# RWKV-6 attention with a mixture-of-depths layer: row shifts issued by ScalarE, another layout of the exponentials, another order on TensorE

## The chip, the cores and the metric

The kernel runs on one core of a Trainium2 chip. The metric is the device time of one launch in microseconds (us), from start to end on that core; lower is better. A profile of one execution lies beside the times. In it PE is TensorE, PEld its weight loads, DVE VectorE, ACT ScalarE, POOL GpSimd, SP SyncE; "L205" is line 205 of the kernel before, and "SPq" is the time that SP's queue spends on issuing DMAs.

## The reference

Two layers follow each other. The first is a linear attention with a decay for each channel (4 batches, 8 heads, 768 steps, 48 channels per head), the second lets the 128 best-scored rows of each batch through a small MLP (384 to 1024 to 384):

```python
for t in range(S):
    cur = np.einsum('bhd,bhe->bhde', u[None] * kt, vt)
    y[:, :, t] = np.einsum('bhd,bhde->bhe', rt, state + cur)
    state = wt[:, :, :, None] * state + np.einsum('bhd,bhe->bhde', kt, vt)
...
scores = np.einsum('bsd,d->bs', x, w_gate)
for b in range(B):
    top_idx = np.argpartition(-scores[b], capacity)[:capacity]
    xe = x[b, top_idx]
    ye = np.maximum(xe @ w1, 0.0) @ w2
    g = 1.0 / (1.0 + np.exp(-scores[b, top_idx]))
    out[b, top_idx] = x[b, top_idx] + g[:, None] * ye
```

Here x is y with the heads side by side: 384 columns.

## The kernel before

**Chunks.** The 768 steps of a batch are cut into 6 chunks of 128 steps, so there are 24 chunks, numbered 0 to 23 over the batches. The 128 steps lie on the partitions. For each chunk `load` (L107) fetches w, k, r and v with one DMA each, 192 KB in runs of 48 numbers.

**What is computed for a chunk.** `lnw` (L137, ACT) takes the logarithm of the decays. `sums` (L146) multiplies it on PE with a triangular matrix, which gives sums from each step to the end of the chunk; ACT then makes `fall` = exp(sum) (L149) and `rise` = exp(-sum) (L160). `scaled` (L205, DVE) needs `rise` for r, and for k it needs `e`: the rows of `fall` moved up by one step. For the first three chunks `e` is made by a second product (L155, L156); for all others two DMAs copy rows 1 to 112 and 113 to 127 of `fall` to the partitions below (L159, issued by SP). `turned` (L216 PE, L218 ACT) transposes k and r; `scores` (L233), `fresh` (L249), `from_state` (L292) and `from_chunk` (L310) are the products proper. They use quarters of the PE array: 16 products of at most 64 x 64 each, twice 16 instructions since fp32 takes two passes. `masked` (L261), `states` (L274 to L281) and `result` (L332, L338, L342) close the chunk on DVE, POOL and SP.

**The whole decay.** The first row of `fall` holds the decay over the whole chunk. The state of the next chunk is scaled by it (L281, POOL), so it has to stand on the partitions, one channel each. `line` (L166) sends that row to DRAM, and `whole` (L174) fetches it back in two DMAs of 48 x 4 single numbers.

**The order.** The program is one loop over turns n = -4 ... 23 (L532), written out by hand; each engine executes its part in the order of the text. One turn works on several chunks: loads of chunk n+7, `sums` of n+4, `scaled` of n+3, `turned` of n+2, `scores` to `states` of n+1, `from_state` and `from_chunk` of n, `result` of n-1. SP's queue in a turn is: four loads, in turns 0 to 6 one DMA with MLP weights (L537), two of `whole`, one of `result` (which waits for DVE's L332), two shifts, one of `line`. All quarter products of a chunk go to one of two PSUM buffers (`ps_p`), so `scores(n+1)` has to wait until `result(n-1)` has read the other use of that buffer. `fall` lies in two buffers in turn, so `fall` of chunk n+4 waits until the DMAs that read `fall` of chunk n+2 are done. In the compiled program the DMAs share eight completion semaphores, and an issue waits until the earlier DMA on its semaphore has landed.

**The MLP.** `mixture` (L347 on) is a generator of 28 steps per batch; while a batch's 6 turns run, the steps of the batch before it are dealt out, 4 or 5 per turn (`per_turn`, L485), half of them after `line` and half at the end of the turn. Steps: two halves of a transposed score row (`every`, L354, L357), six comparisons (`ahead`, L367), the choice of rows and their gather (L376 to L410), the transposed rows (`xeT`, L418, L420), the gate (L425 to L441), eight steps of the first product (L449; after the fourth and eighth, ACT's `hid`, L454), eight of the second (L459, then `ye`, L465). All its PSUM tiles share one buffer (pool `psM`). The MLP of the last batch runs alone at the end (L561).

Of the kernel before, what the change touches and what calls it, by code (L numbers as in the profile page):

```python
# [9 lines left out]
FP32 = mybir.dt.float32  # L10
# [3 lines left out]
AF = mybir.ActivationFunctionType  # L14
# [3 lines left out]
L = 128  # L18
HB = 64
# [17 lines left out]
def kernel(  # L37
# [14 lines left out]
    nc = tc.nc  # L52
# [27 lines left out]
    N = len(chunks)  # L80
    views = dram_disjoint_views(out, B)

    lines = dram.tile([N, C], FP32, name="lines")
    score = consts.tile([L, B, NCH], FP32)
    guard = consts.tile([L, N, 2], FP32)
    w1 = consts.tile([L, NDC, F], FP32)
# [2 lines left out]
    wg_bc = consts.tile([L, C], FP32)  # L89
    k_bufs = [consts.tile([L, H, HB], FP32, name=f"k_buf{i}") for i in range(4)]  # L90
    r_bufs = [consts.tile([L, H, HB], FP32, name=f"r_buf{i}") for i in range(3)]
    e_bufs = [consts.tile([L, C], FP32, name=f"e_buf{i}") for i in range(3)]
    p_bufs = [psP.tile([L, 2, 512], FP32, name=f"ps_p{i}") for i in range(2)]
    all_bufs = [consts.tile([L, HP], FP32, name=f"all_buf{i}") for i in range(6)]

# [37 lines left out]
    def lnw(n):  # L133
        if 0 <= n < N:
# [3 lines left out]
                out=t["lw"], in_=t.pop("w").rearrange("p h d -> p (h d)"), func=AF.Ln  # L138
            )

    def sums(n):
        if not 0 <= n < N:
            return
        t = work[n]
        ps = psR.tile([L, 512], FP32, tag="r", name="ps_x")
        nc.tensor.matmul(ps[:, 0:C], tri, t["lw"], start=True, stop=True)  # L146
        fall = t["fall"] = lev.tile([L, C], FP32, tag="fall", name="fall")
        rise = t["rise"] = lev.tile([L, C], FP32, tag="rise", name="rise")
        after[n - 4] = nc.scalar.activation(  # L149
            out=fall, in_=ps[:, 0:C], func=AF.Exp, accum_out=guard[:, n, 0:1]  # L150
        )
        e = t["e"] = e_bufs[n % len(e_bufs)]
        if n < EARLY:
            strict = psR.tile([L, 512], FP32, tag="r", name="ps_x")
            nc.tensor.matmul(strict[:, 0:C], tri_s, t["lw"], start=True, stop=True)  # L155
            nc.scalar.activation(out=e, in_=strict[:, 0:C], func=AF.Exp)  # L156
        else:
            for lo, hi in ((0, L - 16), (L - 16, L - 1)):
                nc.sync.dma_start(out=e[lo:hi], in_=fall[lo + 1:hi + 1])  # L159
        nc.scalar.activation(  # L160
            out=rise, in_=ps[:, 0:C], func=AF.Exp, scale=-1.0, accum_out=guard[:, n, 1:2]
        )

    def line(n):
        if 0 <= n < N:
            nc.sync.dma_start(out=lines[n:n + 1], in_=work[n]["fall"][0:1])  # L166

    def whole(n):
        if not 0 <= n < N or chunks[n][1] == 0:
            return  # L170
        t = work[n]["all"] = all_bufs[n % len(all_bufs)]
        line = lines[n].rearrange("(j q d) -> q d j", q=2, d=D)
        for par in (0, 1):
            nc.sync.dma_start(out=t[HB * par:HB * par + D, :], in_=line[par])  # L174
# [16 lines left out]
    def own_values(n):  # L191
        if not 0 <= n < N:
            return
        t = work[n]
        t["vo"] = lev.tile([L, H, D], FP32, tag="vo", name="vo")
        nc.gpsimd.tensor_mul(t["vo"], t["v"], t.pop("own").to_broadcast([L, H, D]))  # L196

    def scaled(n):
        if not 0 <= n < N:
            return  # L200
        t = work[n]
        t["K"] = k_bufs[n % len(k_bufs)]
        t["R"] = r_bufs[n % len(r_bufs)]
        for to, of, by in (("K", "k", "e"), ("R", "r", "rise")):
            nc.vector.tensor_mul(  # L205
                t[to][:, :, 0:D], t.pop(of), t.pop(by).rearrange("p (h d) -> p h d", d=D)
            )

    def turned(n):
        if not 0 <= n < N:  # L210
            return
        t = work[n]
        for name in "KR":
            ps = psR.tile([L, HP, L], FP32, tag="r", name="ps_t")
            for j in range(HP):
                nc.tensor.transpose(ps[:, j, :], t[name][:, 2 * j:2 * j + 2, :], ident)  # L216
            t[name + "t"] = lev.tile([L, HP, L], FP32, tag=name + "t", name=name + "t", bufs=3)
            nc.scalar.copy(out=t[name + "t"], in_=ps)  # L218
        t.pop("R")

    quarters = [(par, sub) for par in (0, 1) for sub in (0, 1)]

# [3 lines left out]
    def scores(n):  # L226
        if not 0 <= n < N:
            return
        t = work[n]
        P = t["P"] = p_bufs[n % 2]  # L230
        for j in range(HP):
            for par, sub in quarters:
                nc.tensor.matmul(  # L233
                    P[half(sub), par, j * HB:(j + 1) * HB],
                    t["Kt"][half(par, D), j, half(sub)], t["Rt"][half(par, D), j, half(sub)],
                    start=True, stop=True,
                )
        t.pop("Kt")
# [44 lines left out]
    def from_state(n):  # L283
        if not 0 <= n < N:
            return
        t = work[n]
        begun = set()
        for j in range(HP):
            for par, sub in quarters:
                if sub == 0 and chunks[n][1] == 0:  # L290
                    continue
                nc.tensor.matmul(  # L292
                    t["P"][half(sub), par, j * D:(j + 1) * D],
                    t["Rt"][half(par, D), j, half(sub)],
                    t["s1" if sub else "s0"][half(par, D), j, :],
                    start=(par, sub) not in begun, stop=False, skip_group_check=True,
                )
                begun.add((par, sub))
# [182 lines left out]
    def mix(n):  # L481
        for _ in range(n):
            next(mixing, None)
# [4 lines left out]
    with tc.manual_schedule():  # L488
# [20 lines left out]
        nc.vector.tensor_tensor(out=ident, in0=col, in1=row, op=ALU.is_equal)  # L509
        for t in k_bufs + r_bufs:  # L510
            nc.vector.memset(t[:, :, D:HB], 0.0)
        for t in all_bufs:
            nc.gpsimd.memset(t, 1.0)
        nc.vector.tensor_tensor(out=behind[:, 0:L], in0=col, in1=row, op=ALU.is_lt)
        for i in (0, 1):
            nc.vector.tensor_copy(out=mask[half(i)], in_=behind[half(i), half(i)])
# [15 lines left out]
        for n in range(-4, N):  # L532
            if n > -4:
                load(n + AHEAD)
            if n >= 0 and n < len(weights):
                to, of = weights[n]
                nc.sync.dma_start(out=to, in_=of)  # L537
            whole(n + 3)
            result(n - 1)
            if n > 0 and chunks[n][1] == 0:  # L540
                mixing = run(mixing, mixture(chunks[n][0] - 1))
            pieces = per_turn[chunks[n][1]] if n >= NCH else 0
            lnw(n + 4)
            turned(n + 2)
            from_state(n)
            own_products(n + 3)
            own_values(n + 1)
            sums(n + 4)
            line(n + 4)
            mix(pieces // 2)  # L550
            scaled(n + 3)
            own_sum(n + 2)
            scores(n + 1)
            fresh(n + 1)
            masked(n + 1)
            states(n + 1)
            from_chunk(n)
            mix(pieces - pieces // 2)
        result(N - 1)
        mixing = run(mixing, mixture(B - 1))  # L560
        mix(1000)  # L561
# [81 lines left out]
```

## Time and profile before

| | |
|---|---|
| median of 3 runs | 267.96 us (266.21 to 270.43) |
| the profiled execution | 270.15 us |
| its span in the profile | 268.2 us |
| PE, PEld busy | 198.0, 154.3 us |
| DVE busy | 142.7 us |
| POOL busy | 101.2 us |
| ACT busy | 74.5 us |
| mean granted PE clock | 0.837 of full speed |
| DMA moved | 33.50 MB in 117347 packets, 109491 of them under 512 B |
| K product (L205, DVE) of chunk 3, 9, 15, 21 starts at | 35.53, 83.22, 134.13, 186.13 us |
| last product of the last chunk (L310) ends, about | 231 us |

The busy share of an engine is an average over stages: up to about 84 us the loads and weights fill the DMA queues, then three batches of about 52 us each carry the MLP of the batch before, and from 233 us on the last MLP stands alone. The start times of the K products mark the turns (chunk m is scaled in turn m-3), so they show what each stage costs.

### The profile page before, as it was taken

How to read it: one execution, taken by the hardware profiler on the slowest of the kernel's cores; microseconds unless marked ns; L12 is line 12 of the kernel's file. 1: busy time of each engine (PE TensorE's matmuls, PEld its weight loads, DVE VectorE, ACT ScalarE, POOL GpSimd, SP SyncE). 2: the span in 40 equal slices, each digit the busy share in tenths (PEclk: the TensorE clock that was granted, in tenths of full speed). 3: DMA queues.
4: the chain of work that ended last, by engine and by line, in shares of the span. 5: the costliest groups of instructions: out<-in, count | busy, mean ns of one | idle time of the engine just before them, and what ended most of it. 6: DMA issues, size and time to landing. Idle time of an engine off the chain costs nothing.

```text
span 268.2 us, 8468 instructions
## 1 busy us (share of the span) xinstructions
PE 198.0 (74%) x3592; PEld 154.3 (58%) x3592; DVE 142.7 (53%) x330; ACT 74.5 (28%) x200; POOL 101.2 (38%) x119
## 2 busy tenths in 40 slices
PE   3728557859958859889986698899746988824880
PEld 1416446646747647777765497666535986413740
DVE  7324054345655966576499586566994633271010
ACT  3506313233233312441352134433502110000100
POOL 5350422555414642573175524814735220101001
PEclk9995956795696866999997679999995799955995
DMA  7999779879878867776586746612122001011001
GB/s 146 196 200 200 142 168 229 199 199 240 210 155 199 200 147 166 178 149 139 119 196 151 172 107 144 139 32 91 32 61 62 32 18 46 12 47 33 0 0 42
DMA packets 117347, 33.50 MB, mean 125 GB/s; under 512 B 109491, under 2 KB 116534, under 8 KB 117302
## 3 DMA queue, kind: packets, MB, share of 16 engines
q1 hardware_dynamic: 116790, 31.31, 52.1%
q0 software_dynamic: 512, 1.57, 1.8%
q8 instruction: 30, 0.49, 0.8%
q14 instruction: 15, 0.12, 0.1%
HBM read 23.23 MB, written 5.54 MB: 107 GB/s over the span
## 4 chain that ended last, share of the span: by engine, by line
PE 42%; DVE 17%; SPq 13%; DMA 12%; issue 7%; ACT 5%; POOL 0%; DVEq 0%; POOLq 0%; ACTq 0%
PE ps_f L459 9%; SPq L107 9%; PE ps_h L449 8%; DMA e_buf<-fall 7%; DVE ahead L367 5%; PE ps_p L310 5%; PE ps_t L216 4%; PE ps_x L146 4%; PE ps_p L233 4%; PE ps_p L292 4%; DMA xe<-out_dram,idx 2%; DVE sc L261 2%; PE ps_p L249 2%; SPq L174 2%; ACT rise L160 2%
## 5 line engine op out<-in xcount | busy, mean ns | idle before, releaser
L281 POOL TENSOR_TENSOR s<-mid,all_buf 128x192 f32<-128x192 f32 x20 | 12.1, 603 | 96.3 <-PE ps_p L310 24.5
L205 DVE TENSOR_TENSOR k_buf<-k,e_buf 128x384 f32<-128x384 f32 x24 | 20.8, 868 | 43.6 <-DMA e_buf<-fall 33.4
L218 ACT COPY Kt<-ps_t 128x512 f32<-128x512 f32 x24 | 14.1, 586 | 95.8 <-PE ps_t L216 95.8
L310 PE MATMUL ps_p<-v,sc 64*64 64x48 f32 x768 | 32.9, 240 | 2.7 <-issue 2.5
L261 DVE TENSOR_TENSOR sc<-ps_p,mask 128x512 f32<-128x512 f32 x24 | 16.4, 685 | 32.0 <-PE ps_p L249 32.0
L310 PEld LDWEIGHTS ps_p<-v,sc 64*64 64x64 f32 x768 | 30.4, 157 | 3.8 <-issue 3.4
L146 PE MATMUL ps_x<-lw,tri 128*128 128x384 f32 x48 | 27.9, 670 | 5.7 <-ACT lw L137 5.7
L181 POOL TENSOR_TENSOR rk<-r,k 128x384 f32<-128x384 f32 x24 | 28.6, 1193 | 6.4 <-DVE own L189 4.3
L449 PE MATMUL ps_h<-xeT,w 128*128 128x128 f32 x192 | 27.3, 295 | 3.9 <-ACT hid L454 2.7
L182 POOL TENSOR_TENSOR rk<-rk,u_bc 128x384 f32<-128x384 f32 x24 | 26.3, 1095 | 6.2 <-DMA u_bc<-in_u_dram 4.4
L449 PEld LDWEIGHTS ps_h<-xeT,w 128*128 128x128 f32 x192 | 24.8, 204 | 6.6 <-ACT hid L454 3.2
L459 PE MATMUL ps_f<-w,hid 128*128 128x384 f32 x64 | 23.9, 504 | 3.3 <-ACT hid L454 2.6
L233 PEld LDWEIGHTS ps_p<-Rt,Kt 48*64 48x64 f32 x768 | 16.8, 165 | 16.5 <-issue 9.1
L196 POOL TENSOR_TENSOR vo<-v,own 128x384 f32<-128x384 f32 x24 | 24.4, 1015 | 4.4 <-DVE x L332 4.4
L233 PE MATMUL ps_p<-Rt,Kt 48*64 48x64 f32 x768 | 20.6, 259 | 4.0 <-DVE x L332 4.0
L216 PE MATMUL ps_t<-ident,r_buf 128*128 128x128 f32 x96 | 19.2, 335 | 5.8 <-ACT e_buf L156 5.8
L216 PE MATMUL ps_t<-ident,k_buf 128*128 128x128 f32 x96 | 18.7, 327 | 6.4 <-DVE k_buf L205 6.4
L149 ACT ACTIVATE fall<-ps_x 128x384 f32<-128x384 f32 x24 | 11.8, 490 | 38.1 <-PE ps_x L146 23.8
L292 PE MATMUL ps_p<-s,Rt 48*64 48x48 f32 x704 | 18.5, 242 | 4.1 <-DVE mid L279 4.1
L292 PEld LDWEIGHTS ps_p<-s,Rt 48*64 48x64 f32 x704 | 15.5, 154 | 9.9 <-issue 7.9
L367 DVE SCALAR_TENSOR_TENSOR ahead<-every,score,behind 128x768 bf16<-128x768 f32 (+5 forms) x24 | 19.8, 868 | 1.2 <-ACT every L357 1.2
L205 DVE TENSOR_TENSOR r_buf<-r,rise 128x384 f32<-128x384 f32 x24 | 18.8, 783 | 0.0
(79 smaller groups left out, 263.1 us busy)
## 6 DMA issues: line engine op xcount, KB each, us to landing
w<-in_w_dram SPq DMA_DIRECT2D x24, 192.0 KB
k<-in_k_dram SPq DMA_DIRECT2D x24, 192.0 KB
r<-in_r_dram SPq DMA_DIRECT2D x24, 192.0 KB
v<-in_v_dram SPq DMA_DIRECT2D x24, 192.0 KB
out_dram<-x SPq DMA_DIRECT2D x24, 192.0 KB
e_buf<-fall SPq DMA_DIRECT2D x21, 168.0 KB
w<-in_moe_w_dram SPq DMA_DIRECT2D x3, 512.0 KB
w<-in_moe_w_dram SPq DMA_DIRECT2D x4, 384.0 KB
```

What stands on the lines that cost most here:

```text
L146: nc.tensor.matmul(ps[:, 0:C], tri, t["lw"], start=True, stop=True)
L181: nc.gpsimd.tensor_mul(rk, t["r"], t["k"])
L182: nc.gpsimd.tensor_mul(rk, rk, u_bc)
L196: nc.gpsimd.tensor_mul(t["vo"], t["v"], t.pop("own").to_broadcast([L, H, D]))
L205: nc.vector.tensor_mul(t[to][:, :, 0:D], t.pop(of), t.pop(by).rearrange("p (h d) -> p h d", d=D))
L216: nc.tensor.transpose(ps[:, j, :], t[name][:, 2 * j:2 * j + 2, :], ident)
L233: nc.tensor.matmul(P[half(sub), par, j * HB:(j + 1) * HB], t["Kt"][half(par, D), j, half(sub)], t["Rt"][half(par, D), j, half(sub)], start ...
L292: nc.tensor.matmul(t["P"][half(sub), par, j * D:(j + 1) * D], t["Rt"][half(par, D), j, half(sub)], t["s1" if sub else "s0"][half(par, D), ...
L310: ins = nc.tensor.matmul(t["P"][half(sub), par, j * D:(j + 1) * D], t["sc"][half(sub), par, j, :], t["v"][half(sub), 2 * j + par, :], star ...
L367: nc.vector.scalar_tensor_tensor(out=ahead[:, c, lo:S], in0=every[:, lo:S], scalar=score[:, b, c:c + 1], in1=behind[:, 0:S - lo], op0=ALU. ...
L449: nc.tensor.matmul(ps[:, q, :], w1[:, dc, (f0 + q) * L:(f0 + q + 1) * L], xeT[:, dc, :], start=(dc == 0), stop=(dc == NDC - 1),)
L459: nc.tensor.matmul(ps, hid[:, fc, :], w2[:, fc, :], start=(fc == 0), stop=(fc == NFC - 1))
```

## The change

There are three parts.

1. **Shifts from ScalarE.** The two DMAs that shift `fall` into `e` are issued by ACT, after `rise`; ACT's queue holds them between `rise` and what follows.
2. **Another layout of `fall` and `e`.** Both are stored as [parity of the head, channel, head pair] with 64 channel rows, of which 16 hold ones: a channel's four head pairs lie side by side. Row 0 is then, number by number, what the 128 partitions need, 4 each: `whole` becomes one DMA from SBUF to SBUF of 128 x 4 numbers, with no trip through DRAM, and comes at the end of the same turn in place of `line`. ACT writes `fall` and DVE reads `e` in steps of 16 bytes; a shifted row is two runs of 768 bytes instead of one of 1536. `fall` lies in two fixed buffers.
3. **Another order.** In a turn PE now has: transposes of K, `from_state`, transposes of R, `scores`, `sums`, a third of the MLP steps, `fresh`, a third, `from_chunk`, the rest. Before it was: both transposes, `from_state`, `sums`, half of the steps, `scores`, `fresh`, `from_chunk`, the rest.

```diff
-    lines = dram.tile([N, C], FP32, name="lines")
-    e_bufs = [consts.tile([L, C], FP32, name=f"e_buf{i}") for i in range(3)]
+    fall_bufs = [consts.tile([L, 2, HB, HP], FP32, name=f"fall_buf{i}") for i in range(2)]
+    e_bufs = [consts.tile([L, 2, D, HP], FP32, name=f"e_buf{i}") for i in range(3)]
...
+    def natural(ap):
+        return ap.rearrange("p q d j -> p j q d")
...
         after[n - 4] = nc.scalar.activation(
-            out=fall, in_=ps[:, 0:C], func=AF.Exp, accum_out=guard[:, n, 0:1]
+            out=natural(fall[:, :, 0:D, :]),
+            in_=ps[:, 0:C].rearrange("p (j q d) -> p j q d", q=2, d=D),
+            func=AF.Exp, accum_out=guard[:, n, 0:1],
         )
+        nc.scalar.activation(
+            out=rise, in_=ps[:, 0:C], func=AF.Exp, scale=-1.0, accum_out=guard[:, n, 1:2]
+        )
...
             for lo, hi in ((0, L - 16), (L - 16, L - 1)):
-                nc.sync.dma_start(out=e[lo:hi], in_=fall[lo + 1:hi + 1])
-        nc.scalar.activation(
-            out=rise, in_=ps[:, 0:C], func=AF.Exp, scale=-1.0, accum_out=guard[:, n, 1:2]
-        )
-    def line(n):
-        if 0 <= n < N:
-            nc.sync.dma_start(out=lines[n:n + 1], in_=work[n]["fall"][0:1])
+                nc.scalar.dma_start(out=e[lo:hi], in_=fall[lo + 1:hi + 1, :, 0:D, :])
...
-        line = lines[n].rearrange("(j q d) -> q d j", q=2, d=D)
-        for par in (0, 1):
-            nc.sync.dma_start(out=t[HB * par:HB * par + D, :], in_=line[par])
+        nc.sync.dma_start(out=t, in_=work[n]["fall"][0:1].rearrange("o q d j -> o (q d j)"))
...
+        nc.vector.tensor_mul(
+            t["K"][:, :, 0:D].rearrange("p (j q) d -> p j q d", q=2),
+            t.pop("k").rearrange("p (j q) d -> p j q d", q=2), natural(t.pop("e")),
+        )
...
-        for t in all_bufs:
-            nc.gpsimd.memset(t, 1.0)
+        for t in fall_bufs:
+            nc.gpsimd.memset(t[:, :, D:HB, :], 1.0)
...
-            whole(n + 3)
             result(n - 1)
...
-            turned(n + 2)
+            turned(n + 2, "K")
             from_state(n)
+            turned(n + 2, "R")
             own_products(n + 3)
             own_values(n + 1)
+            scores(n + 1)
             sums(n + 4)
-            line(n + 4)
-            mix(pieces // 2)
+            whole(n + 4)
+            mix(pieces // 3)
             scaled(n + 3)
             own_sum(n + 2)
-            scores(n + 1)
             fresh(n + 1)
             masked(n + 1)
             states(n + 1)
+            mix(pieces // 3)
             from_chunk(n)
-            mix(pieces - pieces // 2)
+            mix(pieces - 2 * (pieces // 3))
```

`turned(n, name)` is the old `turned` for one of the two names.

More of the change, by code (lines that the diff above doesn't have):

```diff
@@ L146, in sums @@
         nc.tensor.matmul(ps[:, 0:C], tri, t["lw"], start=True, stop=True)
-        fall = t["fall"] = lev.tile([L, C], FP32, tag="fall", name="fall")
+        fall = t["fall"] = fall_bufs[n % len(fall_bufs)]
         rise = t["rise"] = lev.tile([L, C], FP32, tag="rise", name="rise")
+        e = t["e"] = e_bufs[n % len(e_bufs)]
         after[n - 4] = nc.scalar.activation(
-            out=fall, in_=ps[:, 0:C], func=AF.Exp, accum_out=guard[:, n, 0:1]
-        )
-        e = t["e"] = e_bufs[n % len(e_bufs)]
+            out=natural(fall[:, :, 0:D, :]),
+            in_=ps[:, 0:C].rearrange("p (j q d) -> p j q d", q=2, d=D),
+            func=AF.Exp, accum_out=guard[:, n, 0:1],
+        )
+        nc.scalar.activation(
+            out=rise, in_=ps[:, 0:C], func=AF.Exp, scale=-1.0, accum_out=guard[:, n, 1:2]
+        )
         if n < EARLY:
@@ L155, in sums @@
             nc.tensor.matmul(strict[:, 0:C], tri_s, t["lw"], start=True, stop=True)
-            nc.scalar.activation(out=e, in_=strict[:, 0:C], func=AF.Exp)
+            nc.scalar.activation(
+                out=natural(e), func=AF.Exp,
+                in_=strict[:, 0:C].rearrange("p (j q d) -> p j q d", q=2, d=D),
+            )
         else:
             for lo, hi in ((0, L - 16), (L - 16, L - 1)):
-                nc.sync.dma_start(out=e[lo:hi], in_=fall[lo + 1:hi + 1])
-        nc.scalar.activation(
-            out=rise, in_=ps[:, 0:C], func=AF.Exp, scale=-1.0, accum_out=guard[:, n, 1:2]
-        )
-    def line(n):
-        if 0 <= n < N:
-            nc.sync.dma_start(out=lines[n:n + 1], in_=work[n]["fall"][0:1])
+                nc.scalar.dma_start(out=e[lo:hi], in_=fall[lo + 1:hi + 1, :, 0:D, :])
     def whole(n):
@@ L203, in scaled, with turned @@
         t["R"] = r_bufs[n % len(r_bufs)]
[L204 to L209, printed above, removed]
+        nc.vector.tensor_mul(
+            t["K"][:, :, 0:D].rearrange("p (j q) d -> p j q d", q=2),
+            t.pop("k").rearrange("p (j q) d -> p j q d", q=2), natural(t.pop("e")),
+        )
+        nc.vector.tensor_mul(
+            t["R"][:, :, 0:D], t.pop("r"), t.pop("rise").rearrange("p (h d) -> p h d", d=D)
+        )
+    def turned(n, name):
         if not 0 <= n < N:
@@ L212, in turned @@
         t = work[n]
[L213 to L219, printed above, removed]
+        ps = psR.tile([L, HP, L], FP32, tag="r", name="ps_t")
+        for j in range(HP):
+            nc.tensor.transpose(ps[:, j, :], t[name][:, 2 * j:2 * j + 2, :], ident)
+        t[name + "t"] = lev.tile([L, HP, L], FP32, tag=name + "t", name=name + "t", bufs=3)
+        nc.scalar.copy(out=t[name + "t"], in_=ps)
     quarters = [(par, sub) for par in (0, 1) for sub in (0, 1)]
```

## Prediction

> **What bounds the kernel now.** I read the page's chain first, then the waits, then the timeline of two engines in one turn, then the busy times by stretch.
>
> The chain of work that ended last says which engines carry the end:
>
> ```profile
> PE 42%; DVE 17%; SPq 13%; DMA 12%; issue 7%; ACT 5%; POOL 0%; DVEq 0%; POOLq 0%; ACTq 0%
> ```
>
> SP's issues and DMA together hold a quarter of it, all before 84 us in order of time; later the chain is PE, with DVE in the first two turns of each batch. So there are two kernels in one: a loading part, and a PE part that starts near 84 us. The waits show what the loading part waits for:
>
> ```profile
> DVE k_buf L205 <- DMA e_buf<-fall: 33.4, 7, 8.8
> ACT fall L149 <- DMA lines<-fall: 8.9, 3, 6.1
> PE ps_f L459 <- ACT hid L454: 2.6, 3, 1.0
> ```
>
> (Total us, times, longest.) DVE waits seven times for the shifted rows, all before 84 us. Why they come late, SP's queue shows (start, duration, DMA, count):
>
> ```profile
> 46.17 0.44 SPq L342 DMA_DIRECT2D out_dram<-x  x1
> 47.12 1.47 SPq L159 DMA_DIRECT2D e_buf<-fall  x2
> 48.65 0.40 SPq L166 DMA_DIRECT2D lines<-fall  x1
> 49.09 0.41 SPq L107 DMA_DIRECT2D w<-in_w_dram  x1
> 50.00 0.78 SPq L107 DMA_DIRECT2D k<-in_k_dram  x1
> 50.82 0.82 SPq L107 DMA_DIRECT2D r<-in_r_dram  x1
> 51.74 0.64 SPq L107 DMA_DIRECT2D v<-in_v_dram  x1
> 52.43 1.33 SPq L537 DMA_DIRECT2D w<-in_moe_w_dram  x1
> 53.86 0.86 SPq L174 DMA_DIRECT2D all_buf<-lines  x2
> 54.76 0.44 SPq L342 DMA_DIRECT2D out_dram<-x  x1
> ```
>
> and on DVE, where the time in brackets is the idle time before and what ended it:
>
> ```profile
> 52.49 0.56 DVE L205 TENSOR_TENSOR k_buf<-k,e_buf 128x384 f32<-128x384 f32 x1 [4.58 <-DMA e_buf<-fall]
> ```
>
> `fall` for this shift started at 41.14; its shift was issued 6 us later, after eight other issues, and landed 5.3 us after that. From 46.17 to 54.76 SP is issuing for 7.15 of 8.59 us. But the transfers themselves are not far from full either (stretch, length, PE, PEld, DVE, ACT, POOL busy, PE clock, DMA share, GB/s):
>
> ```profile
> 36.00:44.00 8.00, 7.52 (x134) 6.01 (x134) 3.27 (x9) 2.63 (x7) 3.61 (x4) 0.50 0.99 223
> 44.00:52.00 8.00, 6.28 (x138) 4.72 (x138) 3.74 (x9) 2.54 (x7) 3.61 (x4) 0.77 0.86 213
> ```
>
> **The change, part by part.** Sums are against the profiled execution: span 268.2, its time 270.15, which is 2.2 above the median.
>
> *Shifts on ACT, start-up.* Chunk 3 is the first with a shift. Its `fall` runs at 24.28, its shift is issued at 32.59 behind loads and `whole`, and K starts at 35.53. With the change `fall` of chunk 2 no longer waits for `line` of chunk 0 (6.06 us idle before it), but `fall` of chunk 3 waits for `whole` of chunk 1, which SP issues after the loads of chunk 4, at about 21.2; `line` took 2.5 (17.60 to 20.10), so `fall` stays at about 24. Then `rise` and two issues (1.47), landing 2.2 after the last (row of chunk 3: issue start 33.28 in the chain, 2.16 to landing): K at 28.5. **-7.0 us.**
>
> *The turns with weights (K of chunk 3 to K of chunk 9).* They take 83.22 - 35.53 = 47.7, or 7.95 each. The shift leaves the loop of DVE's x, SP's queue, the transfer and K. SP's issues fall by 1.47 + 0.40 + 0.86 and gain one `whole`, taken as 0.44 like `out_dram` (128 pieces): 2.3 less, about 5.6 a turn. What is late next? The DMA share in the five 8-us stretches from 36 to 76 is 0.99, 0.86, 0.81, 1.02, 0.79, mean 0.894: 0.894 x 7.95 = 7.1 us of transfers a turn, which the change leaves (the shift's pieces are halved, the 384 single numbers become 128 of 16 bytes). PE at full clock needs, from the turn at 125.30, 0.44 + 0.61 + 0.53 + 0.52 + 0.75 + 0.36 + 1.04 = 4.25, and in this stage sometimes stands for no reason that the profile shows:
>
> ```profile
> 59.77 1.13 PE L310 MATMUL ps_p<-v,sc 64*64 64x48 f32 x30 [1.79 <-issue]
> ```
>
> So PE could go at 6.05, DMA at 7.1. I take 7.1: 6 x (7.95 - 7.1) = **-5.1**. The low end: loads run 7 chunks ahead and are used 3 or 4 turns later, and compute waits for SP only through `whole` of two chunks earlier, so it may gain a turn on the loads; at 6.05 it is 6 x 1.9 = -11.4. The high end is 7.95 again, 0.
>
> *Issues on ACT, in the turns with MLP steps.* They lie behind `rise`; behind them wait `lnw`, then the copies of the transposes, and in some turns `every`, `xeT` or `hid`, on which PE waits because `psM` is one buffer. In turn 9 of before:
>
> ```profile
> 110.58 0.49 ACT L149 ACTIVATE fall<-ps_x 128x384 f32<-128x384 f32 x1 [0.82 <-PE ps_x L146]
> 111.53 0.60 ACT L454 ACTIVATE hid<-ps_h 128x512 f32<-128x512 f32 x1
> 112.18 0.94 PE L449 MATMUL ps_h<-xeT,w 128*128 128x128 f32 x6 [0.96 <-ACT hid L454]
> ```
>
> PE stood 0.96 for `hid`, 0.95 after `fall` began. With the issues between, `hid` comes 1.0 later if they overlap `rise`, 1.45 if not; `fresh` (0.36), now ahead of the next MLP step, covers part: +0.6 to +1.1, taken 0.85. Two such turns in each of the two batches that still have shifts: **+3.4**. No row shows an issue on ACT: below it could be 0.1 each (the queue only hands it over, then -0.3 a turn for the covered part), above 1.5 each, like the slowest shift on SP (1.44), then +2.4 a turn. I take SP's own pair, the same instruction. In the turns of `every` and `xeT` DVE or other PE work hides it; without that cover, another 1 us in each of five turns.
>
> *Order, turn 2 of a batch's MLP (7, 13, 19).* `scores` waits for DVE's x behind three comparisons (PE idle 1.91 before L233 at 143.16). Now `sums` is behind it, so `fresh` and `masked` do not come earlier and one comparison (0.47) moves behind `states`: +0.4 three times, **+1.2**. Turns 20 to 22 have no `sums` and no shift: there `fresh` covers 0.36 of two waits for `hid`, and `scores` (0.95) part of the 1.16 that PE waits for the gathered rows at 206.37: **-1.7**. That quarter products stand apart gains nothing that I can find: `scores`, `fresh`, `from_chunk` in a row take 0.52 + 0.36 + 1.04, and `from_chunk` alone between MLP steps (229.85 to 230.92) takes 1.07 too. Bounds 0 and -0.5 a turn for 17 turns.
>
> *Layout.* ACT writes and DVE reads in steps of 16 bytes; no row has that. The widest like rows bound it: K at 0.56 and, with POOL at work beside it, 1.35, so 0 to 0.8 more. I take 0, as 48-number pieces cost L332 nothing (0.55 for 384 numbers). Where DVE is the bound (two turns a batch, three batches) the upper end is +4.8. [...]
>
> POOL's memsets at the start (0.3) lie before `fall` at 5.91 and stay hidden.
>
> Sum: -7.0 - 5.1 + 3.4 + 1.2 - 1.7 = **-9.2**: span 259.0, its time 261.0, and from the median 267.96 - 9.2 = **258.8 us**.
>
> [...]
>
> **The rivals.**
>
> 1. *PE, not DMA, sets the loading turns.* For it: loads are ahead by 3 turns, the share falls to 0.79 in places. Against: 0.99 and 1.02 in others. Then -11.4 in place of -5.1: 252.5.
> 2. *The loads hold everything.* SP still waits in each turn for `fall` and for x, and its loads for landed predecessors; turns stay near 7.7, the start-up gives 5: -5 - 1.5 + 2.9 = -3.6: 264.4. For it: the DMA share of 0.9 from 1 us on. The shift's own lateness is then replaced by late loads.
> 3. *ACT's queue becomes the wait (slower).* If an issue on ACT takes 1.5 or waits for a landed transfer before it on its semaphore, ACT holds `hid`, `every`, `xeT` and the copies of Kt and Rt in turns 0 to 19. Over the 13 turns 7 to 19, 0.7 us a turn beyond my forecast eats the gain (13 x 0.7 = 9.1), from 1.1 it is slower by 2%; at 1.5 more, 13 x 1.5 = 19.5: 278. For it: the semaphores are shared with SP's loads. Against: ACT is busy 2.6 of 8 us, and the issues on its semaphores are mostly a turn old.
> 4. *The 16-byte steps cost their upper end*: +4.8: 263.6.
>
> **How the numbers follow.** Forecast 0.47 (own range 255 to 262.5), rival 1 0.20, rival 2 0.16, rival 3 0.10, rival 4 0.07. Faster by over 2% (below 262.6; about what a measurement here can tell): 0.47 + 0.20 and some of rivals 2 and 4, 0.71. Within 2%: 0.19. Slower: rival 3, 0.10. The range: below, rival 1 with issues on ACT that cost nothing (252.5 - 3.4 = 249) and a little of the order's bound; above, rivals 2 and 4 together (264.4 + 4.8 = 269): 248 to 268. Rival 3 is left out.
>
> **What would show it.** K of chunk 3 at about 28.5 and of chunk 9 at about 71; no DVE wait for `e` over 1 us after that; SP with gaps in each turn; `hid` starting about 2 us after `fall`, and PE's waits for `hid` about doubled; K still 0.56, `fall` 0.49. From K of chunk 15 to that of chunk 21 the turns should take 54 instead of 52. I am wrong if the loading turns stay at 8 us with a DMA share near 1, if ACT shows idle time before its own shifts, or if L205 grows.

## The result and the profile after

The changed kernel takes 288.93 us (median of 4 runs, 285.04 to 291.26) where the kernel before takes 267.68 us on the same chip. It is slower by 21 us; the forecast was 258.8 us. Some executions of one and the same kernel take over 1.5% longer than its fastest, so that here and below times are medians of all runs, while ratios are of the faster runs alone (of the changed kernel 285.04 and 287.92) and need not be those of the medians beside them. The ratio is 1.072, 95% interval 1.057 to 1.088. The profiled execution took 289.94 us, with a span of 287.1 us and a mean PE clock of 0.765 (before: 268.2 us and 0.837).

The start times of the K products, which mark the turns, say where the time went:

| K product of chunk | before, us | after, us | stage before | stage after |
|---|---|---|---|---|
| 3 | 35.53 | 29.67 | 35.5 | 29.7 |
| 9 | 83.22 | 76.06 | 47.7 | 46.4 |
| 15 | 134.13 | 135.79 | 50.9 | 59.7 |
| 21 | 186.13 | 199.37 | 52.0 | 63.6 |
| end of the span | 268.2 | 287.1 | 82.1 | 87.7 |

The start-up gained what was forecast, nearly. The turns with weights gained 1.3 us instead of 5.1, the two batches of turns with MLP steps lost 8.8 and 11.6 us, and the last stage, which has no shifts any more, lost 5.6. Three views show the first traces of that. First the waits (total us, times, longest), one line of the kernel before and then the changed one:

```profile
PE ps_e L354 <- ACT every L357: 4.1, 4, 1.2
```

```profile
DVE k_buf L207 <- DMA e_buf<-fall_buf: 10.6, 5, 3.3
...
PE ps_e L358 <- ACT every L361: 7.7, 4, 2.8
...
PE ps_h L453 <- ACT hid L458: 4.9, 3, 2.1
PE ps_f L463 <- ACT hid L458: 4.8, 3, 2.1
```

DVE's 33.4 us of waiting for the shifted rows have become 10.6: the shifts do come earlier. (10.2 us more stand before the K product of chunk 3, where before it was 8.8; the view puts them down to a load of w, which that product does not read.) But PE's longest wait for `hid` has gone from 1.0 to 2.1 us, and that for `every` from 1.2 to 2.8. The timeline of ACT in turn 9 shows why (start, duration, then the idle time before in brackets):

```profile
109.34 0.87 ACT L154 ACTIVATE fall_buf<-ps_x 128x384 f32<-128x384 f32 x1 [0.88 <-PE ps_x L150]
...
110.06 0.48 ACT L159 ACTIVATE rise<-ps_x 128x384 f32<-128x384 f32 x1
110.24 0.64 ACTq L171 DMA_DIRECT2D e_buf<-fall_buf  x1
...
110.92 0.90 ACTq L171 DMA_DIRECT2D e_buf<-fall_buf  x1
111.88 0.60 ACT L458 ACTIVATE hid<-ps_h 128x512 f32<-128x512 f32 x1 [1.25 <-issue]
```

`fall` takes 0.87 us where it took 0.49, and the two issues hold ACT's queue from 110.24 to 111.82. `hid` starts 2.54 us after `fall`; before it was 0.95. What such a wait can do to PE stands in its timeline in turn 16, first of the kernel before, then of the changed one:

```profile
174.24 1.09 PE L310 MATMUL ps_p<-v,sc 64*64 64x48 f32 x31
175.26 2.20 PE L459 MATMUL ps_f<-w,hid 128*128 128x384 f32 x6
```

```profile
180.13 0.56 PE L253 MATMUL ps_p<-v,k_buf 64*48 64x48 f32 x16
182.75 1.35 PE L463 MATMUL ps_f<-w,hid 128*128 128x384 f32 x2 [2.06 <-ACT hid L458]
184.04 1.95 PE L314 MATMUL ps_p<-v,sc 64*64 64x48 f32 x32
185.92 4.17 PE L463 MATMUL ps_f<-w,hid 128*128 128x384 f32 x6
```

After 2.06 us without work the 32 products of `from_chunk` take 1.95 us and the six of L463 4.17; before they took 1.1 and 2.20. PE came out of the wait at half clock: the profile has 0.50 from 183.09 to 189.92. The loading turns have a like trace, in the busy times by stretch (length, then PE, PEld, DVE, ACT, POOL busy, PE clock, DMA share, GB/s):

```profile
36.00:44.00 8.00, 7.87 (x137) 6.00 (x137) 4.31 (x9) 2.98 (x7) 3.27 (x5) 0.50 0.81 189
44.00:52.00 8.00, 7.87 (x138) 5.76 (x136) 4.37 (x9) 2.98 (x7) 2.73 (x4) 0.50 0.84 196
```

Here PE is busy for 98% of the time and stays at half clock, and DMA has room (0.81 and 0.84, where before it was 0.99 and 0.86). In this execution, PE has taken SP's place as the late one.

### The profile page after: what moved, and what is told of

It reads as the page before. It is cut to its first block, busy times and chain, and to the rows that moved or that the text cites. A ratio compares the mean times of both kernels' runs of the same rounds, so it can differ in the third digit from the quotient of the medians.

```text
span 287.1 us, 8404 instructions
## 1 busy us (share of the span) xinstructions
PE 223.7 (78%) x3592; PEld 166.6 (58%) x3592; DVE 156.2 (54%) x330; ACT 84.5 (29%) x200; POOL 102.3 (36%) x115
## 5 line engine op out<-in xcount | busy, mean ns | idle before, releaser
L207 DVE TENSOR_TENSOR k_buf<-k,e_buf 128x384 f32<-128x384 f32 x24 | 32.4, 1351 | 25.1 <-DMA e_buf<-fall_buf 10.6
L314 PE MATMUL ps_p<-v,sc 64*64 64x48 f32 x768 | 35.7, 257 | 6.3 <-ACT fall_buf L154 2.9
L150 PE MATMUL ps_x<-lw,tri 128*128 128x384 f32 x48 | 30.7, 732 | 12.4 <-ACT lw L137 12.4
L199 POOL TENSOR_TENSOR vo<-v,own 128x384 f32<-128x384 f32 x24 | 26.7, 1111 | 24.5 <-DVE x L336 22.6
L154 ACT ACTIVATE fall_buf<-ps_x 128x384 f32<-128x384 f32 x24 | 20.8, 867 | 41.7 <-PE ps_x L150 29.2
L185 POOL TENSOR_TENSOR rk<-rk,u_bc 128x384 f32<-128x384 f32 x24 | 30.0, 1248 | 6.0 <-DMA u_bc<-in_u_dram 4.2
L463 PE MATMUL ps_f<-w,hid 128*128 128x384 f32 x64 | 26.9, 549 | 5.0 <-ACT hid L458 4.8
L184 POOL TENSOR_TENSOR rk<-r,k 128x384 f32<-128x384 f32 x24 | 24.3, 1011 | 9.0 <-DVE own L192 6.9
L336 DVE TENSOR_TENSOR x<-ps_p,vo 128x384 f32<-128x384 f32 x24 | 13.3, 553 | 20.7 <-PE ps_p L314 19.4
L253 PEld LDWEIGHTS ps_p<-v,k_buf 64*48 64x48 f32 x704 | 13.6, 151 | 12.5 <-issue 9.3
```

The costliest lines, as they stand in the source:

```text
L154: after[n - 4] = nc.scalar.activation(out=natural(fall[:, :, 0:D, :]), in_=ps[:, 0:C].rearrange("p (j q d) -> p j q d", q=2, d=D), func=AF ...
L207: nc.vector.tensor_mul(t["K"][:, :, 0:D].rearrange("p (j q) d -> p j q d", q=2), t.pop("k").rearrange("p (j q) d -> p j q d", q=2), natura ...
L314: ins = nc.tensor.matmul(t["P"][half(sub), par, j * D:(j + 1) * D], t["sc"][half(sub), par, j, :], t["v"][half(sub), 2 * j + par, :], star ...
L463: nc.tensor.matmul(ps, hid[:, fc, :], w2[:, fc, :], start=(fc == 0), stop=(fc == NFC - 1))
```

## The experiments

In all edits below, "before" and "changed" say which of the two kernels is the base. Ratios are to the kernel before on the same chip, with their 95% interval. "K9" is the start of the K product of chunk 9, and so on. A turn's length is taken from one start of the transposes of K to the next.

### One part at a time

Three theories stood against each other: O, the order on PE; A, the issues on ACT; L, the 16-byte layout.

**Order alone** (before, with the changed loop and `turned` by name; `line` and `whole` as before):

```diff
-            mix(pieces // 2)
+            mix(pieces // 3)
...
-            scores(n + 1)
             fresh(n + 1)
...
+            mix(pieces // 3)
             from_chunk(n)
```

> Only the order of the turn is changed on the kernel before: transposes of K and R apart, scores ahead of sums, the MLP steps in three parts. Shifts on SP, layout and lines as before. Theory O (the order costs: the undisturbed turn 11 grew by 0.63 us warm, more where PE's clock is at half): 16 to 20 such turns are 10 to 13 us, so 278 to 281. Theory A (the issues on ACT cost, by holding hid and every): no change, 268. Theory L (the 16-byte layout costs): 268.

277.84 us, 1.036 (1.030 to 1.042). The order costs 9.7 us by itself. That is about what theory O had, but not by its reason, as the section on the order shows.

**Old order** (changed, with the loop of before):

> The changed kernel with the order of the kernel before: shifts on ACT, 16-byte layout and one transfer for the decay row, but the turn as it was. Theory O: the start-up gain stays and the loss goes, 289 - 13 or better, 262 to 276. Theory A: PE's 2 us waits for hid stay, 285 to 289. Theory L: 285 to 289, with the K product still at 0.85 to 1.4 us.

282.46 us, 1.051 (1.042 to 1.060). This lies between the ranges of the theories. Theory O alone does not hold: without the order most of the loss is still there.

**Issues on ACT alone** (before):

```diff
+        if n >= EARLY:
             for lo, hi in ((0, L - 16), (L - 16, L - 1)):
-                nc.sync.dma_start(out=e[lo:hi], in_=fall[lo + 1:hi + 1])
+                nc.scalar.dma_start(out=e[lo:hi], in_=fall[lo + 1:hi + 1])
```

with `rise` ahead of it.

> Only the shifts are issued from ACT, behind rise; natural layout, the lines through DRAM and the order as before. Theory O: the start-up gain alone, 260 to 264. Theory A: the start-up gain of 6 and about 2 us in every turn with MLP steps, 275 to 285, with PE's waits for hid near 2 us. Theory L: 260 to 264, K at 0.56 and fall at 0.49.

278.29 us, against 268.1. Its four runs are far apart and give no interval: one took 271.34, the others 278.24 to 280.73, and the profile is of the longest. K9 comes at 73.18, 10 us earlier than before, and yet the span of this execution ends 10 us later: the two batches take 59.6 and 61.3 us.

**Layout alone** (changed, old order, shifts back on SP):

> Only the layout of the exponentials (16-byte steps) and the one transfer of the first row; shifts on SP and the order as before. Theory O and theory A: 266 to 269. Theory L: fall 0.38 and K 0.48 longer in up to 23 turns, 275 to 287 if both lie on the path throughout, 270 to 272 if only in the two turns of each batch where DVE is the bound.

271.29 us, 1.013 (1.007 to 1.019). The groups of the two instructions with 16-byte steps, first in the kernel before and then in this one (count, total busy us, mean ns, idle time before):

```profile
L205 DVE TENSOR_TENSOR k_buf<-k,e_buf 128x384 f32<-128x384 f32 x24 | 20.8, 868 | 43.6 <-DMA e_buf<-fall 33.4 <-ACT e_buf L156 10.2
...
L149 ACT ACTIVATE fall<-ps_x 128x384 f32<-128x384 f32 x24 | 11.8, 490 | 38.1 <-PE ps_x L146 23.8 <-DMA lines<-fall 8.9 <-DMA all_buf<-lines 4.5
```

```profile
L207 DVE TENSOR_TENSOR k_buf<-k,e_buf 128x384 f32<-128x384 f32 x24 | 28.1, 1171 | 41.6 <-DMA e_buf<-fall_buf 37.1 <-ACT e_buf L165 4.5
L154 ACT ACTIVATE fall_buf<-ps_x 128x384 f32<-128x384 f32 x24 | 20.8, 866 | 38.2 <-PE ps_x L150 23.4 <-DMA all_buf<-fall_buf 9.5 <-DMA e_buf<-fall_buf 3.4
```

`fall` grows by 0.38 us an execution and the K product by 0.30. The K product grew less than theory L said (0.48), and the time lies in the 270 to 272 that it gave for the case that DVE bounds only two turns of each batch. The run has the one transfer too, so 1.013 is the price of the steps less whatever the transfer saves.

This run and the one with the old order differ only in the engine that issues the shifts, and their intervals lie apart: 282.46 us (1.042 to 1.060) on ACT, 271.29 us (1.007 to 1.019) on SP. So all three parts cost: 1.036, about 1.04 and 1.013 make 1.09, and the changed kernel has 1.072.

### Why do issues on ACT cost 10 us that come 10 us late?

The run with ACT alone has the answer in its timeline of PE, turn 15:

```profile
163.36 0.83 PE L449 MATMUL ps_h<-xeT,w 128*128 128x128 f32 x6
166.33 0.96 PE L449 MATMUL ps_h<-xeT,w 128*128 128x128 f32 x6 [2.13 <-ACT hid L454]
...
168.78 1.89 PE L310 MATMUL ps_p<-v,sc 64*64 64x48 f32 x32
170.60 1.60 PE L449 MATMUL ps_h<-xeT,w 128*128 128x128 f32 x12
```

and, by stretch, the granted clock of the same run (the third number from the right):

```profile
164.60:166.30 1.70, 0.00 (x0) 0.00 (x0) 1.32 (x2) 0.64 (x3) 1.55 (x2) 1.00 0.49 120
166.30:170.60 4.30, 4.27 (x102) 4.07 (x102) 1.31 (x3) 0.39 (x1) 0.06 (x1) 0.60 0.98 188
170.60:174.00 3.40, 3.40 (x55) 3.10 (x54) 3.25 (x5) 1.07 (x2) 3.32 (x4) 1.00 0.17 58
```

In the kernel before, the wait of 0.96 us in the same turn leaves the clock alone:

```profile
163.20:164.20 1.00, 0.04 (x2) 0.02 (x1) 0.50 (x2) 1.00 (x4) 0.73 (x1) 1.00 0.06 7
164.20:167.00 2.80, 2.80 (x103) 2.62 (x103) 0.84 (x2) 0.34 (x1) 0.00 (x0) 1.00 0.45 116
```

The issues make PE's wait longer by 1.2 us, and after the longer wait PE has only half its clock for some 3.4 of the next 4.3 us (the mean of 0.60 says as much); in turns 10 and 16 it is 6.8 us. Turns 9 and 10, 15 and 16 have grown from 8.34 and 8.90 to 9.48 and 13.24, 11.45 and 13.20, and the turns of `every`, 12 and 18, from 6.38 to 9.35 and 9.02: 18.5 us in six turns. One of the four waits for `hid` (2.10 us, turn 9) left the clock at full.

What decides this can be read from the clock record of the traces, which changes only at steps of 3.41 us. Of the twelve waits for `hid` in this run, the changed kernel and the run with the old order (2.05 to 2.56 us each), seven lay with 1.89 us or more in one step, and the clock fell at the end of that step; five were split between two steps, with at most 1.54 us in either, and it did not fall. The same holds over all 18 traces of this case: of the steps at full clock in which PE stood for more than 1.7 us, 147 of 148 were followed by half clock, of those in which it stood for less than 1.2 us, 1 of 561. So a wait of 0.96 us alone is too short, and what a wait of 2.1 us costs depends on where it falls. That the spread of the runs (271.34 to 280.73) comes from this is likely, but not shown.

Theory S from here on: the issues cost only where they stand ahead of `hid` and `every`. Two edits of the kernel before take them away from there.

**ACT only for the early chunks:**

```diff
+            eng = nc.scalar if n < 10 else nc.sync
             for lo, hi in ((0, L - 16), (L - 16, L - 1)):
-                nc.sync.dma_start(out=e[lo:hi], in_=fall[lo + 1:hi + 1])
+                eng.dma_start(out=e[lo:hi], in_=fall[lo + 1:hi + 1])
```

> Shifts issued from ACT only for chunks 3 to 9, that is in turns without MLP steps; from chunk 10 on from SP as before. All else as before. Theory S (what the issues on ACT cost lies in the turns with MLP steps, where hid and every come about 1.1 us later and PE then runs some 4 us at about half clock): K of chunk 9 at about 73 as in the run with ACT alone, later turns as before, so 268 - 10 = 256 to 260. Rival G (what the early turns gain is given back later whatever issues the later shifts): 266 to 270.

264.54 us against 271.28 on this chip, 0.978 (0.969 to 0.986), between the ranges of theory S and rival G.

**ACT for all, but written behind the first half of the MLP steps:**

```diff
             mix(pieces // 2)
+            shift(n + 4)
```

> All shifts issued from ACT, but written behind the first half of the turn's MLP steps, so that hid and every stand ahead of them in ACT's queue. All else as before. Theory S: PE's waits for hid back at about 1.0 us, the cold products after them gone, 256 to 262. Rival Q (the issues hold ACT's queue wherever they lie, and Kt, Rt, lw or fall come late instead): 270 to 280, with PE's or ACT's waits at another place.

265.61 us, 0.980 (0.972 to 0.988). ACT's timeline in turn 10 now has `hid` between `rise` and the second issue, and the second issue in front of nothing that PE waits for:

```profile
110.14 0.49 ACT L149 ACTIVATE fall<-ps_x 128x384 f32<-128x384 f32 x1 [0.82 <-PE ps_x L146]
...
110.62 0.48 ACT L157 ACTIVATE rise<-ps_x 128x384 f32<-128x384 f32 x1
110.86 0.56 ACTq L165 DMA_DIRECT2D e_buf<-fall  x1
...
111.08 0.60 ACT L457 ACTIVATE hid<-ps_h 128x512 f32<-128x512 f32 x1
111.46 0.83 ACTq L165 DMA_DIRECT2D e_buf<-fall  x1
```

`hid` starts 0.94 us after `fall`, PE's longest wait for it is 1.0 us again, and turns 9, 10, 15 and 16 take 8.35, 8.90, 8.34 and 8.90. Theory S holds, rival Q falls: the same issues on the same engine cost nothing a few lines later. All runs of the edit with the issues ahead of `hid` (271.34 to 280.73) lie above all of this one (263.47 to 266.32). Both gains are smaller than expected, though. K9 comes at 69.55 and 70.46 (before 83.22), but K12 only at 101.65 and 99.11 (before 107.65): of 13 us some 6 to 8.5 stay, so part of rival G is right too. In the first of the two runs one reason shows. The shift of chunk 10, on SP again, comes late, and DVE's comparisons stand behind the K product that waits for it (waits, 60 to 90 us):

```profile
PE ps_r L377 <- DVE ahead L368: 7.8, 1, 7.8
...
DVE k_buf L206 <- DMA e_buf<-fall: 8.9, 3, 5.6
```

For the second run the cause is not settled. The DMA share there is 0.92 to 1.03 from 52 to 76 us, so that the loads may be what it runs up against; that is argued, not shown.

**The same move in the changed kernel** (its shift behind the first third of the MLP steps):

```diff
             mix(pieces // 3)
+            shift(n + 4)
```

> The changed kernel, with one thing moved: the two issues of the shift stand behind the first third of the turn's MLP steps on ACT, behind hid and every. Theory S (issues ahead of hid and every cost their time twice, as PE's wait and as half clock after it): the turns of 9.9 to 13.6 us at hid go back to the 8.3 and 8.8 of the run with the order alone, 289 - 10 = 276 to 281. Rival Q (with this order the issues cost at any place): 285 to 290.

276.05 us, 1.044 (1.028 to 1.060), from 1.072; by medians 12.9 us less. Turns 9, 10, 15 and 16 go from 9.87, 10.44, 11.44 and 13.64 to 8.52, 9.08, 8.50 and 9.09, turns 12 and 18 from 8.38 and 9.63 to 6.56: 15.1 us less in these six turns of the profiled executions. Theory S holds in the changed kernel too, by the turns; the two ratios alone would not tell, as their intervals touch (1.057 to 1.088 before the move).

### What does the order cost, and where?

Turn 11 has no wait on PE in any kernel. Before, it took 7.02 us; in the changed kernel it took 7.65. First three groups of the turn before, then the whole turn of the changed kernel:

```profile
129.01 0.69 PE L233 MATMUL ps_p<-Rt,Kt 48*64 48x64 f32 x32
129.53 0.54 PE L249 MATMUL ps_p<-v,k_buf 64*48 64x48 f32 x32
129.89 1.11 PE L310 MATMUL ps_p<-v,sc 64*64 64x48 f32 x32
```

```profile
126.34 0.60 PE L221 MATMUL ps_t<-ident,k_buf 128*128 128x128 f32 x4
126.87 0.68 PE L296 MATMUL ps_p<-s,Rt 48*64 48x48 f32 x32
127.48 0.66 PE L221 MATMUL ps_t<-ident,r_buf 128*128 128x128 f32 x4
128.07 0.69 PE L237 MATMUL ps_p<-Rt,Kt 48*64 48x64 f32 x32
128.70 0.91 PE L150 MATMUL ps_x<-lw,tri 128*128 128x384 f32 x2
129.44 0.81 PE L463 MATMUL ps_f<-w,hid 128*128 128x384 f32 x2
130.18 0.57 PE L253 MATMUL ps_p<-v,k_buf 64*48 64x48 f32 x32
130.69 0.91 PE L463 MATMUL ps_f<-w,hid 128*128 128x384 f32 x2
131.53 1.14 PE L314 MATMUL ps_p<-v,sc 64*64 64x48 f32 x32
132.60 1.56 PE L463 MATMUL ps_f<-w,hid 128*128 128x384 f32 x4
```

The column 128*128 against 48*64, 64*48 and 64*64 is what to read: PE changes between whole-array products and quarter products eight times a turn, and before it was four times (transposes, `from_state`, `sums` and MLP, the three other quarter products, MLP). From start to start, `scores` takes 0.63 us where it took 0.52, `fresh` 0.51 where it took 0.36. Four more changes cost 0.63 us, 0.16 each. Theory X says that this holds for any order.

**`from_state` behind the MLP steps** (before; two changes a turn):

```diff
-            from_state(n)
...
+            from_state(n)
             scores(n + 1)
```

The wait of `from_chunk` is then on the small copy `seen`, as before in chunks 20 to 23.

> Only the order on PE: from_state moved behind the first half of the MLP steps, directly before scores, so that quarter products and full products change places two times a turn and not four; the wait that guards from_chunk is then on a small copy instead of on fall. Theory X (each change between quarter and full products costs PE about 0.15 us; the changed kernel has eight a turn, and its undisturbed turn grew by 0.63): 0.3 less in up to 20 turns, 262 to 266. Rival W (the order cost what it did through waits, not through the changes): 268 or more.

273.28 us against 271.28, 1.005 (1.0005 to 1.010). Turns 9 to 12 take 8.00, 8.56, 6.69 and 6.04, each 0.33 or 0.34 less than before: 0.17 for each of two changes, as theory X has it. The time, however, lies in rival W's range, because other turns of the profiled execution give it back (turns 7, 8 and 14 take 13.10, 12.37 and 11.17 us where they took 10.77, 10.81 and 9.84; PE's waits for DVE's x add up to 7.3 us where it was 4.0).

**K and R apart** (before; only `from_state` between the two transposes):

> Only from_state put between the transposes of K and of R: six changes between quarter and full products a turn. Theory X: 0.3 more in up to 20 turns, 271 to 274, the groups beside the changes each some 0.1 longer. Rival W: 267 to 269.

270.62 us, 1.000 (0.996 to 1.004), and turn 11 takes 6.98 us. The expectation counted wrongly: transposes of R and `sums` are both whole-array products and now stand together, so that the turn still has four changes. Counted rightly, the run agrees with theory X: two changes 0.33 less, four changes 0, eight changes 0.63 more.

So the run with two changes (0.33 or 0.34 us less) and the changed kernel (0.63 us more for eight) put 0.16 to 0.17 us at full clock to one change; what PE does in that time, no trace shows.

The changes are too little for 9.7 us: where PE waits for `hid` anyway, `fresh` ahead of the wait covers it (turns 9 and 10 with the order alone: 8.27 and 8.84, as before). The turn lengths of the order alone show 12.74 us in turn 14 and 15.47 in turn 20, against 9.84 and 10.91. In these the MLP step that transposes the gathered rows stands ahead of `fresh`. It did so before too, but then `scores` also came behind it. Theory P: the cost lies there.

**Third turn of a batch with that step behind `fresh`** (order alone):

```diff
-            mix(pieces // 3)
+            early = 0 if n > 0 and chunks[n][1] == 2 else pieces // 3
+            mix(early)
...
-            mix(pieces // 3)
+            mix(2 * (pieces // 3) - early)
             from_chunk(n)
```

> The order alone, as in the run that took 1.036 of the time before, but in the third turn of each batch the first third of the MLP steps (the transposes of the gathered rows) stands behind fresh instead of ahead of it. Theory P (7.5 of the 9.7 us come from the two turns where PE, just out of the wait for the ranks, meets the gathered rows before its clock is back at full, and then runs 10 us at half clock): 268.5 to 272 on a chip where before takes 268, 1.00 to 1.015. Rival X2 (the eight changes between quarter and full products are the whole cost): 1.03 to 1.04 still.

274.25 us against 268.82, 1.034 (1.015 to 1.054): turns 14 and 20 are shorter as P said (9.93 and 12.44 us), but the time is in rival X2's range, with an interval that begins where P's ends. So both kernels ran again, side by side on one chip.

> The order alone, once more, beside the next run on the same chip: 1.03 to 1.04 by every theory.

> The order alone with the MLP steps of the third turn behind fresh, beside the run before it. Theory P: at least 4 us less than the order alone, 1.00 to 1.02. Rival X2: within 2 us of the order alone.

276.45 us, 1.032 (1.025 to 1.039), for the order alone; 271.82 us, 1.014 (1.006 to 1.021), with the step moved. Theory P holds for 4.6 us, a little over half of the order's cost on this chip, where it had said 7.5; of X2, at most the rest is left. Turn 20 took 15.75 us with the order alone and 12.33 with the step moved. PE's rows there, in this order:

```profile
211.62 0.88 PE L416 MATMUL ps_x<-ident,xe 128*128 128x128 f32 x3 [1.52 <-DMA xe<-out_dram,idx]
...
215.92 1.94 PE L308 MATMUL ps_p<-v,sc 64*64 64x48 f32 x32 [2.60 <-ACT seen L304]
```

```profile
208.12 0.87 PE L416 MATMUL ps_x<-ident,xe 128*128 128x128 f32 x3 [0.29 <-DMA xe<-out_dram,idx]
...
210.42 1.95 PE L308 MATMUL ps_p<-v,sc 64*64 64x48 f32 x32 [1.43 <-ACT seen L304]
```

With `fresh` in the gap PE waits 0.29 us for the gathered rows instead of 1.52. The second wait is one that theory P did not have. `from_chunk` waits here for the small copy `seen`, and in ACT's queue the exponential of the gate stands ahead of that copy; it needs DVE's work on the gathered rows, which in the new order stands behind `masked` and `states`. In the kernel before, the gate comes ahead of `scores`, and PE waits in this turn only 1.16 us for the rows. So PE stands 4.1 us in these two waits with the order alone, 1.7 with the step moved and 1.2 before. Around turn 20 the clock stays at half for 23.9 us with the order alone, 17.1 with the step moved and 10.2 before. No run moves the gate alone, so how the cost splits between the two waits is open.

In turn 14 (10.90 and 10.16 us) there is no wait for `seen`, and the clock is at half for 13.65 us in both runs, only at other times (from 146.3 and from 142.5 us). In the first run of the order alone it was at half from 149.1 us, again for 13.65 us, and turn 14 took 12.74 us: that loss was a matter of when the half clock began.

### The account, and a faster version

**Both moves in the changed kernel:**

> The changed kernel with two things moved: the issues of the shift behind the first third of the MLP steps, and, in the third turn of each batch, that third behind fresh. If theories S and P are the account: 276 less the 6 us of the two turns with gathered rows, 1.00 to 1.02 of the time before, what is left being the layout. If P is not: 1.03 to 1.05, as without the second move.

273.2 us against 268.33, 1.019 (1.011 to 1.028). From 1.072 over 1.044 to 1.019: two moves take back some 14 of the 19 us, so the places of the issues and of the gathered rows are most of the loss. How it splits between the two is less sure, as the intervals of 1.044 and 1.019 nearly meet. What is left, against 0.980 for the kernel with only the issues in their new place, is 0.039: the layout (0.013 alone), the rest of the order (0.014 alone), and about 0.012 that no run has singled out. Turn 20 still takes 13.56 us here, against 10.84 there, with 1.7 us of waiting for `seen`. Another part may be how the clock comes back: in the traces with the new order, 51 of 94 steps at half clock in which PE stood for less than 0.1 us were followed by full clock, in those with the old order 94 of 111. Why is open.

**Natural layout, one transfer** (before, shifts on ACT behind the MLP steps; POOL copies the one row into the order of the transfer):

```diff
+        nc.gpsimd.tensor_copy(
+            out=head[0:1, :, 0:D, :].rearrange("p q d j -> p j q d"),
+            in_=work[n]["fall"][0:1].rearrange("p (j q d) -> p j q d", q=2, d=D),
+        )
+        nc.sync.dma_start(out=t, in_=head[0:1].rearrange("o q d j -> o (q d j)"))
```

> Shifts from ACT behind the first half of the MLP steps, natural layout of the exponentials, and the first row to 128 partitions in one transfer without the lines in DRAM: POOL copies that row alone into the order of the transfer. Theory L (the layout costs on ACT and DVE; the transfer by itself is a gain or nothing): fall at 0.49, K at 0.56, 0.970 to 0.982 of the time before. Rival T (the transfer of 16-byte pieces itself is what costs): 0.99 or more.

267.73 us against 268.82, 1.014 (0.995 to 1.032). Not decided: `fall` is at 0.49 again, but POOL's copy waits seven times, 27.1 us in all and up to 6.4, for the transfer that still reads its buffer, and the gather stands behind it. That one transfer in place of three is worth something is not shown.

**Shifts behind the MLP steps, and `from_state` ahead of `scores` where PE does not wait for DVE:**

```diff
+            late = n > NCH + 2 and chunks[n][1] not in (1, 2)
+            if not late:
+                from_state(n)
...
             mix(pieces // 2)
+            shift(n + 4)
...
+            if late:
+                after.pop(n, None)
+                from_state(n)
             scores(n + 1)
```

> Shifts from ACT behind the first half of the MLP steps, as in the run that took 0.98 of the time before, and from_state directly ahead of scores in those turns where PE does not wait for DVE (from turn 9 on, without the second and third of each batch). Theory X (a change between quarter and full products costs 0.17): 0.34 less in 11 turns, 3.7 less than with the shifts alone, 0.965 of the time before. Rival: the copy that now guards from_chunk, or the lost cover, takes it back, 0.98 or more.

259.91 us against 268.82, 0.977 (0.955 to 0.999), and once more with more runs:

> The version with the shifts on ACT behind the MLP steps and from_state ahead of scores in some turns, for a narrower interval: 0.96 to 0.98 of the time before.

258.27 us against 268.33, 0.963 (0.956 to 0.970): 10 us faster than the kernel before, with the natural layout and four changes a turn, or two. By turns, theory X's 0.34 us shows in turns 10, 11 and 15 to 17 (8.56, 6.70, 8.00, 8.56 and 6.68 us); the turns of `every`, 12 and 18, took 0.3 us more instead, and turn 9 took 9.95 instead of 8.34.

## Why the prediction was wrong

**What bounds the kernel.** That SP's issues and DMA stand in the chain only before 84 us is not quite so: about 14 us of them come later, at 156 to 163, 203 and 234 to 245 us. No term of the sum rests on it.

**Start-up, -7.0.** Right, with its mechanism: `fall` of chunk 3 waits for `whole` as said and starts at 24.62 us, the two issues take 2.1 us instead of 1.47, and K3 starts at 29.67 instead of 28.5: -5.9.

**Turns with weights, -5.1.** With the shifts alone on ACT the six turns take 73.18 - 30.53 = 42.7 us, 7.1 each, as forecast; but there is luck in it. The run with ACT for the early chunks has the same instructions in these turns and took 6.5 a turn, and the one with the shifts behind the MLP steps 6.7, so 7.1 us of transfers are no floor. In the changed kernel the turns take 7.73, with PE at a mean clock of 0.65. The two runs of the changed kernel with the issues moved have the same instructions on each engine in these turns, as no MLP steps are dealt out yet, and took 41.7 and 42.7 us at clocks of 0.83 and 0.74; with the old order and the same shifts and layout they took 72.43 - 30.50 = 41.9 us at 0.83. So the half clock of the profiled execution ate this gain, and the new order by itself does not. The prediction had looked at PE at full clock only. It also took the gain as kept: in the three runs of the old order and layout that had it, K9 came 10.0 to 13.7 us earlier, and 4 to 8 us of that are given back by K12.

**Issues on ACT, +3.4.** This is the step that failed first. The issues were sized nearly right (0.64 and 0.90 against the pair at 1.45 to 1.47), so were their overlap with `rise` and the 2 us from `fall` to `hid` (2.5, as `fall` itself grew). Wrong was the price of a longer wait: it was taken as its own length, 0.85 in four turns. In the run with this part alone it cost 12.9 us in these four turns, since the clock fell in three of them. And the cover that was claimed for `every` is not there: its two turns lost 5.6 us. Rival 3 gave 278 us and the run with this part alone took 278.29, but that agreement is luck: not 1.5 us in thirteen turns, but 3 us in six. Of these 18.5 us, 7.3 are longer waits; the rest goes with five stretches at half clock, 23.9 us in all, that follow them, and part of the loss is set off by the 10 us that K9 had gained. In the changed kernel the same four turns grew by 10.9 us, with the clock falling in two of them.

**Order, +1.2 and -1.7, quarter products apart at 0.** The second step that failed. Bounds of 0 and -0.5 a turn left out that standing apart could cost. The row given as evidence (`from_chunk` alone in 1.07 us) shows that group's own length, and the price stands in the groups beside it: 0.63 us for four changes. The +1.2 did not come: in the first run of the order alone turns 13 and 19 took 0.2 to 0.3 us less than before (turn 7, with 13.60 and 11.35 us in the two runs, does not tell). What was forecast for turns 20 to 22 did not come either; turn 20 became the longest (15.5 us). `scores` was to cover part of the 1.16 us that PE waits for the gathered rows there; the wait grew to 1.5 us or more, and the 2.60 us for `seen` came on top, a wait that the working does not have. This step cost 1.036 as a whole. Moving the step with the gathered rows, which the change leaves ahead of `fresh`, takes 4.6 us of it back.

**Layout, 0 within 0 to 0.8.** A size inside its bounds: 0.30 for the K product, and 0.38 for `fall`, for which no bound had been set. The run with the layout alone took 3.2 us more (1.013), near rival 4's +4.8. The runs price the steps; why they cost this, no run shows.

**The signs it named.** K3 about as said; K9 76 instead of 71; DVE's wait for `e` up to 3.3 where 1 was the limit; `hid` 2.5 us after `fall` and its waits doubled, as said; K at 0.85 and `fall` at 0.87 where 0.56 and 0.49 were to stay; K15 to K21 63.6 instead of 54. The chance of 0.10 for slower, on a single mechanism, was too small: each of the three parts cost time by itself, and for the order and the issues the bounds given did not reach the price.

## What to carry to other kernels

An issue on a compute engine's queue is priced by what stands behind it: moved behind `hid`, the same two issues went from +10 us (+3 in one run of four) to -6. A wait of the matrix engine can be priced twice when it grows past a size that costs it the clock (here from 1.0 to 2.1 us, with the moment deciding), so look at the granted clock in the stretch after each wait that a change makes longer. Group products by array shape, and count the changes of shape in a turn when an order is changed (here 0.16 to 0.17 us each at full clock).

## What the hardware showed that was not expected

- Waits of PE of 2.1 to 2.6 us for `hid` were followed by 3.4 or 6.8 us at half clock in seven cases of twelve, namely where at least 1.89 us lay in one of the 3.41 us steps of the clock; the waits of 0.96 us in turns 9, 10, 15 and 16 of the kernel before were not followed by it.
- A change between whole-array and quarter products costs 0.16 to 0.17 us at full clock (turn 11: 6.69, 7.02 and 7.65 us for two, four and eight changes).
- Steps of 16 bytes take an ACT exponential of 384 numbers a row from 0.49 to 0.87 us, and a DVE product that reads one operand so from 0.56 to 0.85 us.
- A DMA issue of a shift holds ACT's queue for mostly 0.54 (natural layout) to 0.64 us (the other) for 112 rows and 0.83 to 0.90 us for 15 rows, in the profile of the changed kernel at most 0.72 and 1.86, and it can begin while ACT still computes the instruction before it (at 110.24 us in turn 9, where `rise` ends at 110.54).
